# A recurrent attention with an MLP behind it: the first eight units in another order of instructions, loads and PSUM banks

## The chip, the cores and the metric

The kernel runs on one core of a Trainium2 chip. The metric is the device time of one execution in microseconds (us); of several runs the median is given. The engines are TensorE (PE; its weight loads are listed as PEld), VectorE (DVE), ScalarE (ACT), GpSimd (POOL) and SyncE (SP, which here only issues DMAs). Each engine works off its own list of instructions in order; semaphores tie the lists together. DMAs are issued from SP, ScalarE and GpSimd.

## The reference

Two stages. The first is a linear attention with a decaying state, for 4 batches, 8 heads, 768 steps and a head size of 48, in float32. The second is an MLP over the 3072 rows of 384 values that the first gives:

```python
for t in range(S):
    kt, vt, rt = k[:, :, t], v[:, :, t], r[:, :, t]
    cur = np.einsum('bhd,bhe->bhde', u[None] * kt, vt)
    y[:, :, t] = np.einsum('bhd,bhde->bhe', rt, state + cur)
    state = w[None, :, :, None] * state + np.einsum('bhd,bhe->bhde', kt, vt)
x = y.transpose(0, 2, 1, 3).reshape(B * S, H * D)      # 3072 x 384
h = x @ w_in                                            # 384 -> 2048
out = (h * sigmoid(h)) @ w_out                          # 2048 -> 384
```

## The kernel before

The 768 steps are cut into 6 chunks of 128. A unit is one chunk of one batch: 24 units, numbered chunk by chunk, so units 0 to 3 are chunk 0. For each unit the kernel does this:

- It loads r, k and v (192 KB each) into one of eight sets of buffers `rin`, `kin`, `vin` (`ld`, L71; `load`, L77). The heads are padded from 48 to 64 columns there; the pads are set to zero once.
- TensorE transposes r and k into PSUM (`turn`, L262), and VectorE multiplies them by powers of the decay on the way out (`decay_one`, L254: `rT`, `kT`).
- `product_pair` (L274) multiplies k by r for two units together, 64 small matmuls, into the four banks of the two PSUM tiles `att`. VectorE masks them into `am` (`masked`, L289). For odd units the halves are swapped, so `cast_v` (L236), which makes a 16-bit `v16` on ScalarE, also makes the crossed `vx` there.
- GpSimd makes the bonus of the step itself: `ku` = k times u (L209), `rku_f` = r times `ku` (L213); VectorE sums it per head (`bonus_sum`, L222), and GpSimd multiplies v by the sum (`bonus_v`, L227: `vu`).
- `outputs_y` (L295) adds up am times v in PSUM, and from chunk 1 on r times the state. `evict_y` (L332) adds `vu` on VectorE and writes `y16`.
- `outputs_s` (L309) and `state` (L336) bring the state on, with `kc`, the decayed k that GpSimd makes (`decayed_k`, L218), and with `sdec`, the decayed state, also from GpSimd (`decayed_state`, L325).
- `y16` is transposed into `xT`: for units 0 to 5 by TensorE and a copy on ScalarE (`turn_y`, `copy_x`), from unit 6 on by a DMA (`turn_y_dma`, L363).

The MLP works on chunks of 512 tokens. `l1` (L398) is a piece of the first layer: 128 or 256 of the 2048 hidden columns, three matmuls of 512 columns or six of 256, then the Silu on ScalarE into `gT`. `l2` (L420) is a piece of the second layer: four of the 16 matmuls of 384 columns that one batch's output takes; after the fourth piece it is evicted and stored. Pieces, the outputs of the attention and its transposed `y` share four PSUM banks, the tag "moe". The weights come in as four 384 KB pieces of `w_in` and four of `w_out` (16 bit, cast on the way), issued by GpSimd (`ld_win`, L83; `ld_wout`, L88).

The order of the work is written out by hand. For the first eight units, and the MLP of chunk 0, a string `order` (L485) names every step: `T0` is the transpose of unit 0, `A01` the product of 0 and 1, `Y0`, `S0` its outputs, `L0.2` and `G0.2` matmuls and Silu of a first-layer piece, `H0` a piece of chunk 1, `i_q0` and `i_o0` weight loads. Each engine gets its instructions in the order of the string. `4*T0` means four matmuls of zeros (`spin`, L158) ahead of `T0`. The string ends ahead of the product of 6 and 7. From there on, the loop at L518 takes two units at a time and puts pieces of the MLP from a list `fillers` between the attention's steps (`fill`, L448), 16 pieces a turn. The second layer of chunk 0 is the first thing in that list. SP also issues the stores.

The loads stand as follows in the lists: `w` as columns from SP and ScalarE; r0 on SP; k0 on ScalarE; `u`, spread over 128 partitions by the DMA (`u_bc`), on ScalarE; then r1, k1, v0, v1, and r, k, v of units 2 to 7 on SP, each behind the last.

Of the kernel before, what the change touches and what calls it, by code (L numbers as in the profile page):

```python
# [15 lines left out]
def kernel(  # L16
# [76 lines left out]
    def columns(eng, dst, src, j):  # L93
# [3 lines left out]
    w_row = cst.tile([1, HD], FP)  # L97
    ones = cst.tile([1, 128], FP)
# [6 lines left out]
    nc.scalar.dma_start(out=w_row, in_=bass.AP(tensor=w.tensor, offset=0, ap=[[0, 1], [1, HD]]))  # L105
    ld(0, rin, r)
    ld(0, kin, k, nc.scalar)
    nc.scalar.dma_start(out=u_bc, in_=bass.AP(tensor=u.tensor, offset=0,
                                              ap=[[0, 128], [D, H], [1, D]]))
    ld(1, rin, r)  # L110
    ld(1, kin, k)
    ld(0, vin, v)
    ld(1, vin, v)
    load(2)
    load(3)
# [25 lines left out]
    for i in range(NIN):  # L141
        nc.gpsimd.memset(kc[i][:, :, D:64], 0.0)
# [9 lines left out]
    def pads():  # L152
        for i in range(B, NIN):
            for dst in (rin, kin):
                nc.scalar.copy(out=dst[i][:, :, D:64],
                               in_=idle[:, 0:128].rearrange("p (h d) -> p h d", h=H))

    def spin(n):  # L158
        zs = ps.tile([128, 512], FP, name="zs", tag="moe", bufs=4)
        for _ in range(n):  # L160
            nc.tensor.matmul(zs, idle[:, 0:128], idle, start=True, stop=True)

    def clear():
        for t in att:
            for y in range(2):
                nc.tensor.matmul(t[:, y, :], idle[:, 0:128], idle, start=True, stop=True)
# [16 lines left out]
    def spread_w():  # L183
        spread["w"] = ps.tile([128, HD], FP, name="bc", tag="moe", bufs=4)
        nc.tensor.matmul(spread["w"], ones, w_row, start=True, stop=True)
# [4 lines left out]
    def powers_c():  # L190
        nc.scalar.activation(out=lamC.rearrange("p h d -> p (h d)"), in_=lnw_bc,
                             func=AF.Exp, scale=it_rev)
        nc.scalar.activation(out=wCT, in_=lnwT, func=AF.Exp, scale=float(C))
        nc.scalar.preload_act_table_set("silu_and_others")
# [14 lines left out]
    def bonus_ku(i):  # L209
        L(i)["ku"] = wrk.tile([128, H, D], FP, name="ku")  # L210
        nc.gpsimd.tensor_tensor(out=L(i)["ku"], in0=kin[i % NIN][:, :, 0:D], in1=u_bc, op=ALU.mult)  # L211

    def bonus_rku(i):  # L213
        L(i)["rku_f"] = wrk.tile([128, H, D], FP, name="rku_f")
        nc.gpsimd.tensor_tensor(out=L(i)["rku_f"], in0=rin[i % NIN][:, :, 0:D], in1=L(i)["ku"],  # L215
                                op=ALU.mult)
# [5 lines left out]
    def bonus_sum(i):  # L222
        L(i)["rku"] = wrk.tile([128, H], FP, name="rku")
        nc.vector.tensor_reduce(out=L(i)["rku"], in_=L(i)["rku_f"],  # L224
                                axis=mybir.AxisListType.X, op=ALU.add)

    def bonus_v(i):  # L227
        L(i)["vu"] = wrk.tile([128, H, D], FP, name="vu")
        nc.gpsimd.tensor_tensor(out=L(i)["vu"], in0=vin[i % NIN],  # L229
                                in1=L(i)["rku"].unsqueeze(2).broadcast_to([128, H, D]),  # L230
                                op=ALU.mult)
# [4 lines left out]
    def cast_v(i):  # L236
        v16 = L(i)["v16"] = L(i)["vy"] = wrk.tile([128, H, D], F16, name="v16", bufs=4)
        nc.scalar.copy(out=v16, in_=vin[i % NIN])  # L238
        if crossed(i):
            vx = L(i)["vy"] = wrk.tile([128, H, D], F16, name="vx", bufs=2)  # L240
            nc.scalar.copy(out=vx[0:HC], in_=v16[HC:C])
            nc.scalar.copy(out=vx[HC:C], in_=v16[0:HC])
# [10 lines left out]

    def decay_one(i, x):  # L254
        key, lam = (("rT", lamR), ("kT", lamK))[x]
        L(i)[key] = wrk.tile([PR, NP, C], FP, name=key)
        nc.vector.tensor_tensor(  # L257
            out=L(i)[key].rearrange("p g (y t) -> p y g t", y=2),
            in0=L(i)["t"][0:PR, :, x], in1=lam.rearrange("p g (y t) -> p y g t", y=2),
            op=ALU.mult)  # L260
# [34 lines left out]
    def outputs_y(i):  # L295
        sc, b = unit(i)
        yp = ps.tile([128, 512], FP, name="yp", tag="moe", bufs=4)
        L(i)["y"] = yp[:, 0:HD].rearrange("p (h d) -> p h d", h=H)
        for p in range(NP):
            if sc:  # L300
                nc.tensor.matmul(L(i)["y"][:, 2 * p:2 * p + 2, :],  # L301
                                 L(i)["rT16"][0:PR, p, :],
                                 st16[b][:, p, :], start=True, stop=False)
            for j in range(2):
                h = 2 * p + j
                nc.tensor.matmul(L(i)["y"][:, h, :], L(i)["am"][:, j, p, :], L(i)["vy"][:, h, :],  # L306
                                 start=not sc, stop=(not sc or j == 1))
# [24 lines left out]
    def evict_y(i):  # L332
        L(i)["y16"] = wrk.tile([128, H, D], F16, name="y16")
        nc.vector.tensor_tensor(out=L(i)["y16"], in0=L(i)["y"], in1=L(i)["vu"], op=ALU.add)  # L334
# [68 lines left out]

    def l2_mm(sc, b, part):
# [6 lines left out]
    def store(sc, b):  # L411
        osb = wrk.tile([128, HD], FP, name="osb", bufs=3)
        if sc < NCH - 1:
            nc.scalar.copy(out=osb, in_=opss[b])  # L414
        else:
            nc.vector.tensor_copy(out=osb, in_=opss[b])
        tt = b * S + sc * C
        nc.sync.dma_start(out=out[tt:tt + C, :], in_=osb)
# [34 lines left out]
    def second(sc):  # L453
        return [lambda b=b, p=p: l2(sc, b, p) for b in range(B) for p in range(4)]

    def rest_first(sc):
        return [lambda ft=ft: l1(sc, 2, 2, ft) for ft in range(0, NFT, 2)]

    def first(sc):
        return [lambda f=f: l1(sc, 0, B, f) for f in range(NFT)]  # L460
# [5 lines left out]
    def piece(word, f):  # L466
# [4 lines left out]
        "lnw": powers_r, "eK": exponents_k, "lamK": powers_k,  # L471
        "wb": spread_w,
        "lnwb": ln_w, "lamC": powers_c, "mx": cross_mask, "pads": pads, "clear": clear,
    }
    unit_steps = {
        "T": turn,
        "rT": lambda i: decay_one(i, 0), "kT": lambda i: decay_one(i, 1),
        "am": masked, "v16": cast_v, "kc": decayed_k,
        "vu": bonus_v,
        "Y": outputs_y, "S": outputs_s, "y16": evict_y, "yT": turn_y, "xT": copy_x,  # L480
        "st": state, "stb": state16, "ku": bonus_ku, "ru": bonus_rku, "rd": bonus_sum,
        "r16": cast_r, "sd": decayed_state, "i_q": ld_win, "i_o": ld_wout,
        "lr": lambda i: ld(i, rin, r), "lk": lambda i: ld(i, kin, k), "lv": lambda i: ld(i, vin, v),
    }
    order = """  # L485
        lnw eK lamK mx clear lr4 lk4 lv4 lr5 lk5 lv5 lr6 lk6 lv6 lr7 lk7 lv7 4*T0 ku0 rT0 kT0
        4*T1 rT1 kT1 v160 ru0 rd0 ku1 wb v161 A01 ru1 am0 rd1 vu0 lnwb i_q0 lamC pads am1 vu1
        4*Y0 y160 T2 kT2 2*Y1 y161 ku2 ru2 rT2 yT0 xT0 i_q1 yT1 xT1 v162 T3 kT3 rT3 ku3 ru3 rd2
        v163 4*A23 vu2 i_q2 rd3 vu3 am2 am3 L0.0 G0.0 L0.2 G0.2 Y2 y162 Y3 y163 kc0 yT2 xT2 L0.4
        G0.4 kc1 yT3 xT3 L0.6 G0.6 S0 st0 kc2 T4 kT4 rT4 kc3 L2.0 G2.0 S1 L2.2 G2.2 st1 ku4 v164  # L490
        L2.4 G2.4 S2 L2.6 G2.6 st2 ru4 i_q3 r164 L4.8 G4.8 S3 L4.9 G4.9 st3 rd4 ku5 L4.10 G4.10
        T5 kT5 rT5 L4.11 G4.11 vu4 ru5 i_o0 A45 rd5 am4 r165 v165 L4.12 G4.12 vu5 kc4 L4.13
        G4.13 am5 sd4 kc5 Y4 S4 y164 st4 L4.14 G4.14 sd5 i_o1 Y5 S5 y165 st5 L4.15 G4.15 yT4 xT4
        yT5 xT5 T6 kT6 rT6 ku6 ru6 i_o2 H0 H1 v166 r166 H2 H3 T7 kT7 rT7 ku7 i_o3 v167 r167 H4
        ru7 rd6 stb4 stb5
    """
    for word in order.split():
        if "*" in word:
            n, word = word.split("*")
            spin(int(n))  # L500
        if word[0] == "A":
            product_pair(int(word[1]))
        elif word in steps:
            steps[word]()
        elif word[0] == "L":
            piece(word[1:], l1_mm)
        elif word[0] == "G":
            piece(word[1:], l1_silu)
        elif word[0] == "H":
# [3 lines left out]
    load(8)  # L513
    load(9)
    fillers.extend([lambda ft=ft: l1(1, 0, 2, ft) for ft in range(10, NFT, 2)])
    fillers.extend(second(0))

    for i in range(B + 2, NU, 2):  # L518
        sc, b = unit(i)
        nxt = range(i + 2, min(i + 4, NU))  # L520
        product_pair(i)
        if i > B + 2:
            for n in nxt:
                bonus_products(n)
                decayed_k(n)
        if i > B + 2:
            masked(i)
            masked(i + 1)
        else:
            bonus_v(i)  # L530
            decayed_k(i)
            decayed_state(i)
            masked(i)
            bonus_sum(i + 1)
            masked(i + 1)
            bonus_v(i + 1)
            decayed_k(i + 1)
            decayed_state(i + 1)
            for n in nxt:
                bonus_products(n)  # L540
                decayed_k(n)
        fill(4)
# [11 lines left out]
        if b:  # L554
            fillers.extend((first(sc) if sc > 1 else rest_first(sc)) + second(sc))
# [46 lines left out]
```

## Time and profile before

| | us |
|---|---|
| median of 5 runs | 194.95 |
| lowest, highest | 194.43, 197.03 |
| the five runs | 197.03, 196.82, 194.43, 194.74, 194.95 |
| the profiled execution | 197.03 |
| its span, first to last instruction | 195.2 |
| mean granted TensorE clock | 0.983 |

All the profile's lines are of the one profiled execution. Its views are read like this. The page gives busy time of each engine, with its share of the span and the number of its instructions, and then the span in 40 slices of 4.9 us, where a digit is the busy share in tenths; PEclk is the clock that TensorE was granted, in tenths. The chain of waits goes back from the last instruction, at each step to what released it; its rows are start, length, engine and line, and "issue" is time in which the engine waited for nothing that the profile shows. A row of groups has line, engine, operation, result and operands, count, busy time and mean ns of one. For a DMA the trace has the issue and the time to landing.

The landing times of the first loads, from issue and time to landing, are these (us):

| load | issue | landed |
|---|---|---|
| r0 (SP) | 1.43 | 4.9 |
| k0 (ScalarE) | 2.00 | 5.9 |
| `u_bc` (ScalarE) | 2.44 | 8.4 |
| r1 | 1.9 | 8.6 |
| k1 | 2.52 | 9.3 |
| v0, v1 | 3.41, 6.0 | 10.1, 10.9 |
| r2, v2 | 8.54, 10.04 | 12.3, 14.2 |
| k4, k5 | 15.32, 20.74 | 21.5, 28.8 |
| k7 | 30.77 | 38.5 |
| `w_in` pieces | 13.30, 18.72, 22.70, 30.17 | 19.5, 23.8, 28.4, 36.3 |
| `w_out` pieces | 36.73, 41.80, 44.66, 46.43 | 41.8, 48.7, 51.5, 54.8 |

### The profile page before, as it was taken

How to read it: one execution, taken by the hardware profiler on the slowest of the kernel's cores; microseconds unless marked ns; L12 is line 12 of the kernel's file. 1: busy time of each engine (PE TensorE's matmuls, PEld its weight loads, DVE VectorE, ACT ScalarE, POOL GpSimd, SP SyncE). 2: the span in 40 equal slices, each digit the busy share in tenths (PEclk: the TensorE clock that was granted, in tenths of full speed). 3: DMA queues.
4: the chain of work that ended last, by engine and by line, in shares of the span. 5: the costliest groups of instructions: out<-in, count | busy, mean ns of one | idle time of the engine just before them, and what ended most of it. 6: DMA issues, size and time to landing. Idle time of an engine off the chain costs nothing.

```text
span 195.2 us, 5626 instructions
## 1 busy us (share of the span) xinstructions
PE 185.3 (95%) x2306; PEld 119.7 (61%) x2306; DVE 102.7 (53%) x188; ACT 108.4 (56%) x212; POOL 120.3 (62%) x159
## 2 busy tenths in 40 slices
PE   7598989889999999999999999999999999999994
PEld 2365776567866786665556665556665556644563
DVE  6248769784663663772772782772673364200120
ACT  5285558758653286067684076792186791179300
POOL 8287995899999957938929919929829430000000
PEclk9966999999999999999999999999999999999999
DMA  4999999999839629349359158359278111320022
GB/s 82 174 201 186 199 196 169 184 203 194 129 82 178 187 52 213 104 106 181 84 111 217 56 126 169 80 97 208 60 161 187 24 20 44 81 81 0 3 81 81
DMA packets 90267, 24.35 MB, mean 125 GB/s; under 512 B 83329, under 2 KB 90242, under 8 KB 90242
## 3 DMA queue, kind: packets, MB, share of 16 engines
q1 hardware_dynamic: 84992, 20.39, 48.2%
q0 software_dynamic: 3712, 3.15, 11.0%
q10 hardware_dynamic: 1538, 0.46, 1.4%
q8 instruction: 18, 0.29, 0.6%
q14 instruction: 7, 0.06, 0.1%
HBM read 20.65 MB, written 4.72 MB: 130 GB/s over the span
## 4 chain that ended last, share of the span: by engine, by line
PE 75%; POOL 13%; issue 4%; DMA 3%; ACT 2%; ACTq 0%; DVE 0%; POOLq 0%
PE ops L408 31%; PE hps L387 26%; PE att L284 7%; PE att L251 4%; POOL ku L211 3%; DMA u_bc<-in_u_dram 3%; POOL kc L219 3%; POOL rku_f L215 2%; POOL vu L229 2%; PE yp L306 2%; PE yp L301 2%; POOL win L84 2%; PE sp L318 1%; PE ops L433 1%; ACT gT L395 1%
## 5 line engine op out<-in xcount | busy, mean ns | idle before, releaser
L387 PE MATMUL hps<-xT,win 128*128 128x512 f16 (+1 forms) x360 | 68.2, 337 | 0.7 <-ACT xT L376 0.5
L395 ACT ACTIVATE gT<-hps 128x512 f16<-128x512 f32 x96 | 56.2, 598 | 20.0 <-PE hps L387 17.9
L408 PE MATMUL ops<-wout,gT 128*128 128x384 f16 x368 | 64.0, 326 | 0.0
L408 PEld LDWEIGHTS <-gT 128*128 128x128 f16 x368 | 34.7, 98 | 22.2
L387 PEld LDWEIGHTS <-win 128*128 128x128 f16 x360 | 33.2, 98 | 24.2 <-issue 1.1
L229 POOL TENSOR_TENSOR vu<-vin,rku 128x384 f32<-128x384 f32 x24 | 19.8, 829 | 30.6 <-DVE rku L224 27.3
L414 ACT COPY osb<-ops 128x384 f32<-128x384 f32 x20 | 9.6, 478 | 43.4 <-PE ops L408 39.7
L291 DVE TENSOR_TENSOR am<-att,maskM 128x1024 f16<-128x1024 f32 x12 | 14.7, 1224 | 35.2 <-PE att L284 35.2
L211 POOL TENSOR_TENSOR ku<-kin,u_bc 128x384 f32<-128x384 f32 x24 | 24.1, 1006 | 3.5 <-DMA u_bc<-in_u_dram 3.3
L215 POOL TENSOR_TENSOR rku_f<-rin,ku 128x384 f32<-128x384 f32 x24 | 24.1, 1004 | 1.7
L219 POOL TENSOR_TENSOR kc<-kin,lamC 128x384 f16<-128x384 f32 x24 | 23.9, 1001 | 0.0
L284 PEld LDWEIGHTS att<-rT,kT 48*64 48x64 f32 x768 | 19.1, 140 | 6.4 <-issue 4.5
L257 DVE TENSOR_TENSOR rT<-att,lamR 112x512 f32<-112x512 f32 x24 | 16.4, 684 | 12.0 <-PE att L251 4.4
L284 PE MATMUL att<-rT,kT 48*64 48x128 f32 (+1 forms) x768 | 21.8, 257 | 1.0 <-DVE rT L257 0.8
L334 DVE TENSOR_TENSOR y<-yp,vu 128x384 f16<-128x384 f32 x24 | 13.3, 556 | 14.1 <-issue 4.8
L257 DVE TENSOR_TENSOR kT<-att,lamK 112x512 f32<-112x512 f32 x24 | 16.4, 681 | 3.6 <-PE att L251 3.5
L291 DVE TENSOR_TENSOR am<-att,maskX 128x1024 f16<-128x1024 f32 x12 | 14.6, 1214 | 0.0
L238 ACT CAST v<-vin 128x384 f16<-128x384 f32 x24 | 11.4, 511 | 4.4 <-DMA vin<-in_v_dram 4.4
L329 POOL TENSOR_TENSOR sdec<-st,wCT 112x384 f32<-112x384 f32 x16 | 13.2, 826 | 0.0
L224 DVE TENSOR_REDUCE rku<-rku_f 128x8 f32<-128x384 f32 x24 | 12.3, 542 | 0.6 <-POOL rku_f L215 0.6
L272 ACT CAST rT<-rT 112x512 f16<-112x512 f32 x20 | 12.4, 619 | 0.3 <-DVE rT L257 0.2
L306 PEld LDWEIGHTS <-am 128*128 128x128 f16 x192 | 10.0, 98 | 3.9 <-DVE am L291 1.7
(64 smaller groups left out, 161.3 us busy)
## 6 DMA issues: line engine op xcount, KB each, us to landing
rin<-in_r_dram SPq DMA_DIRECT2D x24, 192.0 KB, 3.8
vin<-in_v_dram SPq DMA_DIRECT2D x24, 192.0 KB, 4.2
kin<-in_k_dram SPq DMA_DIRECT2D x23, 192.0 KB, 4.0
out_dram<-osb SPq DMA_DIRECT2D x23, 192.0 KB, 2.2
win<-in_moe_w_in_dram POOLq DMA_DIRECT2D x4, 384.0 KB, 5.9
wout<-in_moe_w_out_dram POOLq DMA_DIRECT2D x4, 384.0 KB, 6.9
xT<-y SPq DMA_TRANSPOSE x18, 2.3
kin<-in_k_dram ACTq DMA_DIRECT2D x1, 192.0 KB, 3.9
```

The source lines that it names most:

```text
L211: nc.gpsimd.tensor_tensor(out=L(i)["ku"], in0=kin[i % NIN][:, :, 0:D], in1=u_bc, op=ALU.mult)
L215: nc.gpsimd.tensor_tensor(out=L(i)["rku_f"], in0=rin[i % NIN][:, :, 0:D], in1=L(i)["ku"], op=ALU.mult)
L219: nc.gpsimd.tensor_tensor(out=kc[i % NIN][:, :, 0:D], in0=kin[i % NIN][:, :, 0:D], in1=lamC, op=ALU.mult)
L229: nc.gpsimd.tensor_tensor(out=L(i)["vu"], in0=vin[i % NIN], in1=L(i)["rku"].unsqueeze(2).broadcast_to([128, H, D]), op=ALU.mult)
L257: nc.vector.tensor_tensor(out=L(i)[key].rearrange("p g (y t) -> p y g t", y=2), in0=L(i)["t"][0:PR, :, x], in1=lam.rearrange("p g (y t) -> ...
L284: nc.tensor.matmul(a[e][o0:o0 + HC, j, p, c0:C], kT[r0:r0 + D, p, s0:s0 + HC], rT[r0:r0 + D, p, c0:C], start=True, stop=True)
L291: nc.vector.tensor_tensor(out=am.rearrange("p h g c -> p (h g) c"), in0=L(i)["a"].rearrange("p h g c -> p (h g) c"), in1=(maskX if crossed ...
L306: nc.tensor.matmul(L(i)["y"][:, h, :], L(i)["am"][:, j, p, :], L(i)["vy"][:, h, :], start=not sc, stop=(not sc or j == 1))
L334: nc.vector.tensor_tensor(out=L(i)["y16"], in0=L(i)["y"], in1=L(i)["vu"], op=ALU.add)
L387: nc.tensor.matmul(hps[:, f, :], win[:, q, (ft + f) * 128:(ft + f + 1) * 128], xts[sc][:, q, b0:b0 + nb, :].rearrange("p b t -> p (b t)"), ...
L395: nc.scalar.activation(out=gts[sc][:, ft:ft + m, b0 * C:(b0 + nb) * C], in_=hpss[b0, ft], func=AF.Silu)
L408: nc.tensor.matmul(opss[b], gts[sc][:, ft, b * C:(b + 1) * C], wout[:, ft, :], start=(ft == 0), stop=(ft == NFT - 1))
```

## The change

The order of the first eight units is new, and with it what can stand there.

- Loads: `u` comes as one row and is spread by a matmul, like `w`. The string itself names every load. r, k and v of units 0 to 5 come first; then all the weights; r, k and v of units 6 to 9 come behind a memset on GpSimd that writes into r6's buffer (`hold_rows`), so that SP's next load has to wait for it.
- Order: the products of 0 and 1, 2 and 3, 4 and 5 all stand ahead of the MLP but for one piece. The string now also has the whole second layer of chunk 0 (`M`), and ends behind the product of 6 and 7.
- PSUM: chunk 0's second layer adds up in the banks of `att` (`front_mm`). r and k of units 2, 3, 6 and 7 are transposed into the four "moe" banks (`turn_ring`), r and k apart.
- Units 0 to 3: `vu` is added by a float32 matmul with the identity (`add_bonus`) into a PSUM bank that a matmul of zeros opens, and ScalarE evicts (`evict_y`).
- Small things: `spin` is gone, `clear` has six zero matmuls in place of four. The pads of `kc` are set by VectorE, in the string, and no longer by GpSimd ahead of it; those of `rin` and `kin` 4 to 7 by GpSimd, no longer by ScalarE. The table load for Silu is a step of its own. More buffers for `ku`, `rku_f`, `rku`, `vu`, `v16`, `vx`, `rT`, `kT`, `y16` and `osb`.
- In the loop: the casts of units 6 and 7 stand in its first turn, and the first layer goes by pairs of batches (256 columns) in every chunk, added to `fillers` each turn.

```diff
-    nc.scalar.dma_start(out=w_row, in_=bass.AP(tensor=w.tensor, offset=0, ap=[[0, 1], [1, HD]]))
-    ld(0, rin, r)
-    ld(0, kin, k, nc.scalar)
-    nc.scalar.dma_start(out=u_bc, in_=bass.AP(tensor=u.tensor, offset=0,
-                                              ap=[[0, 128], [D, H], [1, D]]))
-    ld(1, rin, r)
-    ld(1, kin, k)
-    ld(0, vin, v)
-    ld(1, vin, v)
-    load(2)
-    load(3)
+    for dst, src in ((u_row, u), (w_row, w)):
+        nc.scalar.dma_start(out=dst, in_=bass.AP(tensor=src.tensor, offset=0, ap=[[0, 1], [1, HD]]))
+        if src is u:
+            ld(0, rin, r)
+            ld(0, kin, k, nc.scalar)
...
-    for i in range(NIN):
-        nc.gpsimd.memset(kc[i][:, :, D:64], 0.0)
+    for i in range(B, NIN):
+        nc.gpsimd.memset(rin[i][:, :, D:64], 0.0)
+        nc.gpsimd.memset(kin[i][:, :, D:64], 0.0)
...
+    def kc_pads():
+        for i in range(NIN):
+            nc.vector.memset(kc[i][:, :, D:64], 0.0)
+
+    def hold_rows(i):
+        nc.gpsimd.memset(rin[i][:, :, 32:64], 0.0)
...
     def clear():
-        for t in att:
-            for y in range(2):
-                nc.tensor.matmul(t[:, y, :], idle[:, 0:128], idle, start=True, stop=True)
+        for n in range(6):
+            zeros(att[n % 4 // 2][:, n % 2, :])
...
+    def copy_u():
+        nc.vector.tensor_copy(out=u_bc.rearrange("p h d -> p (h d)"), in_=spread["u"])
...
+    def turn_ring(i, x):
+        t = L(i)["t", x] = ps.tile([128, NP, C], FP, name="tr", tag="moe", bufs=4)
+        flat = (rin, kin)[x][i % NIN].rearrange("p h d -> p (h d)")
+        for p in range(NP):
+            nc.tensor.transpose(t[0:PR, p, :], flat[:, 128 * p:128 * p + PR], ident)
...
+        if not sc:
+            nc.tensor.matmul(L(i)["yf"], idle[:, 0:128], idle[:, 0:HD], start=True, stop=False)
...
+    def add_bonus(i):
+        nc.tensor.matmul(L(i)["yf"], ident, L(i)["vu"].rearrange("p h d -> p (h d)"),
+                         start=False, stop=True)
...
+        if i < B:
+            nc.scalar.copy(out=L(i)["y16"], in_=L(i)["y"])
+        else:
+            nc.vector.tensor_tensor(out=L(i)["y16"], in0=L(i)["y"], in1=L(i)["vu"], op=ALU.add)
...
+    def front_acc(b):
+        return att[b // 2][:, b % 2, 0:HD]
+
+    def front_mm(b, part):
+        for ft in range(4 * part, 4 * part + 4):
+            nc.tensor.matmul(front_acc(b), gts[0][:, ft, b * C:(b + 1) * C], wout[:, ft, :],
+                             start=(ft == 0), stop=(ft == NFT - 1))
...
+    def second(sc, b0):
+        return [lambda b=b, p=p: l2(sc, b, p) for b in (b0, b0 + 1) for p in range(4)]
+
+    def first(sc, b0, f0=0):
+        return [lambda ft=ft: l1(sc, b0, 2, ft) for ft in range(f0, NFT, 2)]
...
     order = """
+        clear lr1 lk1 lk2 lnw lk3 eK ub lv0 lv1 lamK lr2 mx lr3 Tr0 ubc Tr1 lr5 rT0
+        Tk0 ku0 lv5 Tk1 rT1 lr4 ku1 kT0 Tk2 lv3 lv2 kT1 ru0 lk4 kT2 A01 ku2 lk5 rd0
+        lv4 kcm ru1 v161 wb q0 am0 Tr2 v160 vu0 lnwb am1 Y0 ku3 lamC Tk3 Tr3 rT2 ru2
+        V0 v165 kT3 Y1 ru3 rT3 silu rd1 A23 kc0 rd2 rd3 vu1 y160 v162 am2 vu2 V1 v163
+        yT0 vu3 am3 Y2 V2 q1 y161 T4 y162 kc1 yT1 xT0 rT4 T5 xT1 kT4 Y3 kc4 S0 V3 rT5
+        q2 yT2 y163 kT5 L0.2 q3 st0 yT3 G0.2 A45 o0 r165 xT2 kc2 S1 r164 L0.0 st1 o1
+        xT3 L0.4 G0.0 kc3 L2.0 v164 S2 G0.4 L0.6 o2 st2 G2.0 L2.2 ku4 G0.6 L2.6 G2.2
+        sd6 S3 L2.10 G2.6 st3 ru4 L2.8 G2.10 L2.4 sd7 rd4 L0.10 G2.4 am5 o3 L4.12 G2.8
+        sd4 L4.13 G4.12 am4 G0.10 L0.8 ku5 G4.13 L4.15 kc5 G0.8 Y4 S4 G4.15 M2.0 st4
+        ru5 Y5 M1.0 stb4 rd5 S5 sd5 M0.0 M2.1 vu4 st5 M3.0 stb5 y164 M0.1 hold6 vu5
+        lr6 M1.1 lk7 y165 L4.14 lk6 M1.2 G4.14 lr7 yT4 lk8 M1.3 lv7 M0.2 lk9 ku7 M0.3
+        lv6 M2.2 lv9 osb0 ku6 lv8 M2.3 lr8 ru7 yT5 Tr6 Tk6 xT5 lr9 xT4 kc6 M3.1 rT6
+        osb1 osb2 Tr7 Tk7 rd7 kT6 vu7 M3.2 rT7 ru6 M3.3 kT7 H0 osb3 rd6 A67
     """
...
-    load(8)
-    load(9)
-    fillers.extend([lambda ft=ft: l1(1, 0, 2, ft) for ft in range(10, NFT, 2)])
-    fillers.extend(second(0))
+    fillers.extend(first(1, 0, 2) + second(1, 0))
...
-        product_pair(i)
         if i > B + 2:
-            for n in nxt:
-                bonus_products(n)
-                decayed_k(n)
+            product_pair(i)
...
+        if i > B + 2:
+            fill(4)
+        else:
+            for n in (i, i + 1):
+                cast_v(n)
+                cast_r(n)
+                fill(2)
...
-        if b:
-            fillers.extend((first(sc) if sc > 1 else rest_first(sc)) + second(sc))
+        fillers.extend(first(sc, b) + second(sc, b))
```

## The prediction

> **What bounds the kernel now.** I read the page's first two parts, then the chain of waits in order of time, then busy times in stretches of 2 us, then each DMA's issue with its time to landing.
>
> ```profile
> span 195.2 us, 5626 instructions
> PE 185.3 (95%) x2306; PEld 119.7 (61%) x2306; DVE 102.7 (53%) x188; ACT 108.4 (56%) x212; POOL 120.3 (62%) x159
> ...
> PEclk9966999999999999999999999999999999999999
> ```
>
> TensorE looks busy for 95% of the span, but that counts the zero products of `spin` and matmuls at half clock. The chain shows where TensorE really sets the pace:
>
> ```profile
> 2.44 5.88 DMA u_bc<-in_u_dram
> ...
> 8.46 0.99 POOL ku L211
> ...
> 32.00 2.95 issue
> 34.99 0.83 POOL vu L229
> ...
> 48.32 1.55 PE att L284 x54
> 49.88 2.07 PE hps L387 x18
> 51.95 0.65 PE ops L408 x4
> ...
> 56.31 1.04 PE att L251 x32
> ...
> 171.54 10.40 PE hps L387 x48
> 181.93 7.80 PE ops L408 x48
> 189.73 2.65 PE ops L433 x32
> ```
>
> Up to 41 us the chain runs over GpSimd, which starts at 8.46 because `u_bc` lands late. From 48.32, the product of units 6 and 7, to 192.4 it is TensorE without a gap: 144.1 us, then 2.8 us of eviction and store. So there are two questions: how much TensorE work is left when that product starts, and when it starts.
>
> ```profile
> 10.00:12.00 2.00, 1.82 (x22) 1.04 (x25) 1.66 (x3) 1.60 (x4) 1.92 (x3) 0.81 1.07 211
> 12.00:14.00 2.00, 2.00 (x52) 1.89 (x44) 0.00 (x0) 1.93 (x5) 2.00 (x3) 0.50 0.95 183
> 14.00:16.00 2.00, 2.00 (x13) 0.84 (x12) 1.87 (x3) 1.99 (x6) 0.32 (x2) 0.50 1.06 170
> 16.00:18.00 2.00, 2.00 (x24) 1.28 (x22) 2.00 (x3) 0.71 (x4) 1.92 (x3) 0.50 1.09 168
> 18.00:20.00 2.00, 1.45 (x32) 1.08 (x30) 1.16 (x3) 0.97 (x3) 1.98 (x3) 0.99 1.23 240
> ```
>
> Columns: stretch, its length, busy PE, PEld, DVE, ACT, POOL (instructions), granted clock, DMA share, GB/s. From 11.2 to 18 the clock is half although TensorE is busy all the time; it comes back after spins at 14.0 and 17.2.
>
> **Work behind the product of 6 and 7.** A first-layer piece is 0.65 us (48 matmuls of 512 columns in 10.40; by pairs, 12 of 256 columns in 1.31, so 0.655), a second-layer piece of four matmuls 0.65. After the change all 16 second-layer pieces of chunk 0 lie ahead of it (-10.4), four of the five early first-layer pieces of chunk 1 fall behind it (+2.6), and 64 pieces go by pairs (+0.3): 144.1 - 7.5 = 136.6. So the product may start at 48.3 + 7.5 = 55.8 without loss; each us later is a us lost.
>
> **The loads.** In the trace r0 lands at 4.9 and v2, the tenth transfer, at 14.2: 1.03 us each. `u` now comes as one 1.5 KB row, spread by a matmul (0.91, the row of `bc`) and a VectorE copy (0.56), both beside idle engines. So the first `ku` starts at 6.0, when k0 is there, not 8.46. In the new order v5 is the 12th and k5 the 17th transfer: 4.9 + 11 x 1.03 = 16.3 and 21.4. The first weight load, issued by GpSimd at about 12, puts 1.9 us between (384 KB at the 205 GB/s that weights alone reach at 48 to 51 us), the second some of the same: v5 at 18.3, k5 between 23.4 and 25.
>
> **The spins.** 18 zero products of `spin` go (6.7 us busy), `clear` gets two more. Those in TensorE's waits gave nothing but the clock. Without them I expect half clock from about 8 us. A product of two units then takes 2.8 us (60 matmuls in 2.83 at 11.26) in place of 1.5, two units' turns 2.2 in place of 1.04. The trace doesn't show when the clock returns without spins: between 13 us and the first window filled by the MLP, some 5 us after its start. I take the middle twenties, since the new bonus products use all rows.
>
> The Trainium skill ("TensorE: Matmul & The Clock Gate", Part 1) has the full clock granted after one busy window of about 3.4 us. The rows speak against it as it stands: 2.00 of 2.00 busy from 12 to 16 us at 0.50. By the rule the clock would be back by 18 and the product of 6 and 7 would start near 54.5; by the rows as below.
>
> **New work on TensorE.** Four bonus products (`add_bonus`, 384 columns, f32): the trace has this shape only in `bc`, 0.91 with its latency; bounds 0.65 and 1.8; I take 0.65 at full and 1.3 at half clock. They wait for GpSimd's `vu`, with turns and outputs queued behind on TensorE; `vu` of 0 to 3 end at 13.8, 18.6, 19.4 and 20.2, each before TensorE gets there, so the wait costs nothing. Four zero matmuls ahead of the outputs: 0.16 to 0.32 each. ScalarE evicts those four units (0.48 each) in place of VectorE (0.56). The pads of `kc` go from GpSimd (1.23 in all) to VectorE, between the first bonus sum and the first mask, where VectorE waits for the product anyway; without that cover they cost 1.2. The pads of `rin`, `kin` go from ScalarE (15.0 to 16.7) to GpSimd, idle there until 6.0.
>
> **Walk to the MLP.** Tk2 ends at 9.7, the product of 0 and 1 at half clock at 12.6, w's spread and r2's turn at 14.0, Y0 at 15.0 (ScalarE casts v0 until 14.2), turns of unit 3 and the bonus at 17.5, Y1 at 18.3, the product of 2 and 3 at 21.1 (19 at full clock). On ScalarE v5's cast and crossing (18.3 to 19.9) and the table load (1.28) stand ahead of y0's eviction: 21.7. Queued behind it are v2's and v3's casts with crossing, then y1's eviction at 24.3. TensorE waits for these in yT0, Y2, yT1 and for k5 in T5. With full clock from 25, T5 ends at 26.3, and Y3, S0, the last bonus, yT2, a first-layer piece, yT3 and the product of 4 and 5 (0.45 + 0.25 + 0.65 + 0.35 + 0.65 + 0.35 + 1.5 = 4.2) give 30.5.
>
> **MLP to the product of 6 and 7.** 15 first-layer pieces 9.8, 16 second-layer pieces 10.4, five state products 0.85, two outputs 0.76, turns 1.4, one piece of chunk 1 0.65: 23.85, so 54.35 if nothing waits. Weights don't: GpSimd issues them at about 20, 23, 24, 25, 26, 28 and 38, and at 1.9 us each all but the last are there by 36; the last lands by 43 to 46 (5.1 to 8.4 to landing in the trace) and is used at 47.7. The banks of `att` don't: the last `osb` copy (0.48) lies beside the piece of chunk 1. GpSimd does: the state evictions of unit 3 (four at 0.32) end at 36.7, then come 0.83 + 0.8 + 0.83 + 3 x 1.0 + 0.5 + 0.83 + 0.83 + 0.5 + 0.2 up to the memset of `hold_rows`: 45. SP's first load of chunk 1's second half waits for it, and all loads and the four stores are queued behind. r6 lands at 48.9 (3.8), r7 third after it at 51.9. GpSimd's `rku_f` of 7 ends at 52.9, VectorE's sum at 53.5, then three decays at 0.61: the product starts at 55.4.
>
> **Behind it.** The casts of units 6 and 7 (v16 0.51 twice, crossing 1.02, rT16 0.62 twice) now stand between ScalarE's Silus of the loop's first pieces; before, ScalarE had them behind it by 48. Four pieces take TensorE 2.6 us; with four PSUM buffers the fifth waits for the third's Silu, behind 3.3 us of casts and three Silus of 0.6. I take a stall of 1.5, bounds 0 and 2.2. Later iterations have nine pieces and the turns (6.9 us) between an output and its first use, against five and 4.4 before with no wait: nothing.
>
> **Sum.** 55.4 + 1.5 + 136.6 + 2.8 = 196.3 us, 1.1 over the span. The profiled execution took 197.03, 1.83 over its span and 2.08 over the median of the five runs (194.43 to 197.03, in two groups). Taken as it stands the sum gives 198.1; as a difference to the median, 196.1. What made the profiled run longer the trace doesn't tell; I take the middle, 197.1.
>
> **Rivals.**
> Faster: the clock is back by 18 and rows land at 0.75 us, as the four from r1 to v1 did (8.6 to 10.9, three steps in 2.25). k5 is there by 21 (16.9, and two weight loads at 1.9), the product of 4 and 5 ends at 28, the one of 6 and 7 starts at 52, ScalarE's stall is hidden: 52 + 136.6 + 2.8 = 191.4, so 193.2 or 191.3, in the middle 192.3. It decides from a start before 53.5. For it: GpSimd starts 2.5 us sooner and the weights come 6 to 15 us sooner. Against: the clock rows, and 190 GB/s shared with the weights.
>
> Much slower: the clock returns only inside the MLP. The walk at half clock: bonus products 1.3, turns 1.1, outputs 0.85 each, the product of 4 and 5 from 32.2 to 35.0, then 23.85 and at least one us of slow MLP: 60. Span 60 + 1.5 + 136.6 + 2.8 = 200.9, so 202.7 or 200.7, about 201.7. For it: 11.2 to 14.7, a whole product and 0.6 us of spin, did not bring the clock back.
>
> No effect: TensorE waits in T5, but sooner (29), GpSimd's chain moves with it, the stall is half: 54 + 0.7 + 136.6 + 2.8 = 194.1, so 195.9 or 193.9, about 194.9.
>
> **How the numbers follow.** About 1% is what a measurement of this kernel can tell from no change. Forecast 0.38 (own range 195.3 to 199; 0.24 of it slower, 0.14 within 1%), much slower 0.24, no effect 0.14 (0.09 within, 0.05 faster), faster 0.24 (0.20 faster, 0.04 within). Together faster 0.25, within 0.27, slower 0.48. A range from 191.8 to 202.5 leaves a tenth at each end.
>
> **What would show it.** The start of the product of 6 and 7 against 55.8; the granted clock in 8 to 30 us; k5's landing and the end of the product of 4 and 5 against 30.5; r7's landing against 51.9 and what ends the wait of that product (a decay, if GpSimd's chain is late); ScalarE's Silus and TensorE's idle just behind it. I would be wrong if that product starts before 53.5, or if the later iterations wait for `xT`.

## The result, and the profile after

The changed kernel took 196.76 us (median of 43 runs, 195.68 to 197.47), the kernel before 195.24 beside it (80 runs, 193.93 to 197.37): a ratio of 1.0078, 95% interval 1.0063 to 1.0093. It is 0.8% slower, less than the 1% that the prediction set as what can be told apart. The prediction was 197.1 (191.8 to 202.5). All ratios leave out the executions that took over 1.5% more than the fastest of the same kernel.

The profiled execution took 197.4 us, with a span of 195.6. These are the lines of its page that answer to those of before:

```profile
span 195.6 us, 5942 instructions
...
PE 188.9 (97%) x2476; PEld 143.8 (74%) x2476; DVE 102.1 (52%) x193; ACT 110.2 (56%) x208; POOL 120.7 (62%) x160
...
PEclk9999999999999999999999999999999999999999
```

The clock's row shows no cut. The chain of waits of the same execution, in order of time (start, length, engine, line):

```profile
9.56 3.42 PE att L293 x62
12.98 1.57 PE bc L180 x2
...
17.98 1.28 PE yp L322 x2
...
19.90 1.72 PE att L293 x64
...
27.82 1.50 PE att L293 x64
...
53.33 0.67 PE hps L406 x6
54.04 0.47 issue
54.51 0.48 ACT osb L445
55.04 1.57 PE att L293 x64
...
58.06 0.60 ACT gT L414
58.66 0.41 ACT v L238
59.09 0.51 ACT vx L241
59.61 0.51 ACT vx L242
60.14 0.62 ACT rT L281
60.76 0.51 ACT gT L414
61.31 0.82 PE hps L406 x6
...
190.04 2.65 PE ops L464 x32
```

Three things are to be seen. GpSimd, which carried the chain up to 41 us before, is gone from it: from 9.56 on the chain is TensorE (94% of the span in all), but for one mask on VectorE at 21.64 and the two holes below. Its first product takes 3.42 us, not 1.5, and a bonus product 1.28, where later ones take 0.73: TensorE runs at half speed up to about 20 us. Of the 3.42, 0.6 are a wait inside the product: its weight loads go on at 10.15, when VectorE has k of unit 1 decayed. The other 2.83 are the time of the half-speed product in the kernel before. And behind dense work up to 54 us there are two holes, both made by ScalarE: the output copy `osb` ahead of the product of units 6 and 7, and the casts of 6 and 7 behind it.

TensorE's busy time in the same stretches of 2 us as before (stretch, its length, busy PE, PEld, DVE, ACT, POOL, granted clock, DMA share, GB/s):

```profile
10.00:12.00 2.00, 2.00 (x40) 1.85 (x40) 1.75 (x11) 1.23 (x3) 2.00 (x3) 1.00 1.11 219
12.00:14.00 2.00, 2.00 (x32) 1.28 (x28) 0.97 (x1) 0.81 (x2) 1.98 (x4) 1.00 1.15 193
14.00:16.00 2.00, 2.00 (x13) 1.29 (x13) 1.76 (x3) 1.20 (x3) 1.93 (x3) 1.00 1.13 173
16.00:18.00 2.00, 2.00 (x15) 2.00 (x13) 1.00 (x2) 1.60 (x4) 0.80 (x1) 1.00 0.97 184
18.00:20.00 2.00, 2.00 (x15) 0.97 (x18) 1.98 (x4) 1.69 (x2) 0.75 (x1) 1.00 0.82 163
```

TensorE is busy throughout and the granted clock says 1.00, yet the instructions take twice their later time. The column is no proof of full speed; the durations are.

The product of 6 and 7 starts at 55.04, before the break-even of 55.8. Behind it lie 137.65 us of TensorE to 192.69, then 2.9 us. By these two profiles the kernels are as good as equal (spans of 195.6 and 195.2); the medians are 1.5 us apart.

### The profile page after: what moved, and what is told of

It is laid out like the page before. It is cut to its first block, busy times and chain, and to the rows that moved or that the text cites. A ratio compares the mean times of both kernels' runs of the same rounds, so it can differ in the third digit from the quotient of the medians.

```text
span 195.6 us, 5942 instructions
## 1 busy us (share of the span) xinstructions
PE 188.9 (97%) x2476; PEld 143.8 (74%) x2476; DVE 102.1 (52%) x193; ACT 110.2 (56%) x208; POOL 120.7 (62%) x160
## 4 chain that ended last, share of the span: by engine, by line
PE 94%; ACT 2%; DVE 2%; issue 1%; DVEq 0%
PE hps L406 32%; PE ops L439 26%; PE att L293 10%; PE att L251 6%; PE att L428 5%; PE yp L318 3%; PE tr L258 2%; PE yp L313 2%; PE sp L334 2%; PE bc L180 2%; PE att L157 1%; PE yp L322 1%; PE ops L464 1%; DVE rT L266 1%; DVE am L300 1%; ACT gT L414 1%
## 5 line engine op out<-in xcount | busy, mean ns | idle before, releaser
L406 PE MATMUL hps<-xT,win 128*128 128x256 f16 (+1 forms) x564 | 70.0, 275 | 0.6 <-DVE y L353 0.5
L406 PEld LDWEIGHTS <-win 128*128 128x128 f16 x564 | 53.2, 98 | 9.2 <-issue 0.9
L439 PE MATMUL ops<-wout,gT 128*128 128x384 f16 x304 | 52.4, 326 | 0.0
L439 PEld LDWEIGHTS <-gT 128*128 128x128 f16 x304 | 29.1, 98 | 18.1
L353 DVE TENSOR_TENSOR y<-yp,vu 128x384 f16<-128x384 f32 x20 | 11.1, 557 | 16.2 <-PE yp L318 5.4
L266 DVE TENSOR_TENSOR rT<-att,lamR 112x512 f32<-112x512 f32 x20 | 13.7, 686 | 9.6 <-PE att L251 9.5
L445 ACT COPY osb<-ops 128x384 f32<-128x384 f32 x16 | 7.6, 478 | 17.9 <-PE ops L439 17.9
L266 DVE TENSOR_TENSOR kT<-att,lamK 112x512 f32<-112x512 f32 x20 | 13.5, 679 | 0.0
L364 DVE TENSOR_TENSOR st<-sp,sdec 48x192 f32<-48x192 f32 x32 | 11.2, 351 | 2.6 <-POOL kc L219 1.6
L373 POOL CAST stb<-st 112x384 f16<-112x384 f32 x16 | 8.1, 505 | 7.2 <-DVE st L364 7.0
```

The costliest lines, as they stand in the source:

```text
L266: nc.vector.tensor_tensor(out=L(i)[key].rearrange("p g (y t) -> p y g t", y=2), in0=L(i)["t"][0:PR, :, x], in1=lam.rearrange("p g (y t) -> ...
L406: nc.tensor.matmul(hps[:, f, :], win[:, q, (ft + f) * 128:(ft + f + 1) * 128], xts[sc][:, q, b0:b0 + nb, :].rearrange("p b t -> p (b t)"), ...
L439: nc.tensor.matmul(opss[b], gts[sc][:, ft, b * C:(b + 1) * C], wout[:, ft, :], start=(ft == 0), stop=(ft == NFT - 1))
```

## The experiments

Theory from this profile: the change takes TensorE's waits for GpSimd away and pays for it at three places: `osb` 1.06, casts 0.9, and the half clock. Rivals: the bonus products' time, the held-back rows, or GpSimd's chain, each of which might set the end as well. Ratios are to the kernel before on the same chip; the changed kernel's own is 1.0078.

**The copy ahead of the product.** In the string, `H0` stands for matmuls and Silu, so the copy behind it in ScalarE's list waits for the Silu:

```diff
-        osb1 osb2 Tr7 Tk7 rd7 kT6 vu7 M3.2 rT7 ru6 M3.3 kT7 H0 osb3 rd6 A67
+        osb1 osb2 Tr7 Tk7 rd7 kT6 vu7 M3.2 rT7 ru6 M3.3 kT7 osb3 H0 rd6 A67
```

> Only the last output copy of chunk 0 (osb3) moves ahead of the first-layer piece H0 in the order; the changed kernel's ratio to before is 1.0078. Theory (TensorE is the bound, and its wait of 1.06 us ahead of the product of 6 and 7 is the copy queued behind H0's Silu on ScalarE): the product starts at 54.0 in place of 55.0 and the time falls by 0.8 to 1.1 us, ratio 1.003. Rival A (GpSimd's chain behind the held loads is just as late): the decays of 7 end the wait instead, the gain is under 0.3 us, ratio 1.007. Rival B (the casts behind the product eat it): the product starts a microsecond sooner, but the sixth piece waits a microsecond longer, ratio 1.007.

195.74 us, ratio 1.0025 (0.9998 to 1.0052): 1.0 us less than the changed kernel. ScalarE's instructions in the changed kernel show why (start, length, line, operation, in brackets the idle time and its releaser):

```profile
51.19 0.48 ACT L445 COPY osb<-att 128x384 f32<-128x384 f32 x1 [0.28 <-PE att L428]
54.02 0.60 ACT L414 ACTIVATE gT<-hps 128x512 f16<-128x512 f32 x1 [2.35 <-PE hps L406]
54.51 0.47 ACT L445 COPY osb<-att 128x384 f32<-128x384 f32 x1
```

ScalarE idles for 2.35 us waiting for the piece, while the sum that the copy needs is ready at about 53.3. With the copy first, TensorE runs without a gap from 52.40 into the product at 53.15. From the start of the product of 4 and 5 to this one lie 26.15 us, 27.28 in the changed kernel. The loss is the order of two instructions on an idle engine.

**The casts.**

```diff
-        osb1 osb2 Tr7 Tk7 rd7
+        osb1 osb2 r166 v167 Tr7 Tk7 rd7
...
-            for n in (i, i + 1):
-                cast_v(n)
-                cast_r(n)
-                fill(2)
+            cast_v(i)
+            cast_r(i + 1)
+            fill(4)
```

> Only the cast and crossing of v7 and the cast of rT6 move from the loop's first turn to ScalarE's idle time ahead of H0. Theory (ScalarE's casts between the first Silus stall TensorE behind the product of 6 and 7): the idle of 0.9 us between 56.6 and 62.0 goes, time -0.6 to -0.9 us, ratio 1.004. Rival (the wait only moves, to v6 or to the state): under 0.3 us, ratio 1.007.

196.17, ratio 1.0043 (1.0016 to 1.0070): 0.6 us less. From the product's start to the next turns TensorE now needs 8.0 us (53.68 to 61.69) in place of 8.9; `osb` still costs 1.06. The span of this profile is 193.3, 2.3 below the changed kernel's, and only 0.9 of that are the casts. The rest comes from the front: TensorE is back at full speed at about 17.4, not 20 (the transpose of r3 at 16.92 takes 0.80 us, 1.06 in the changed kernel), so the product of 4 and 5 starts at 26.40, not 27.76. Nothing was changed there; the moment moves from execution to execution. So what an edit is worth has to be read within one profile, or from many times.

**Both.** The two diffs together.

> Both edits together: osb3 ahead of H0, and v16, vx of 7 and rT16 of 6 cast ahead of the loop. Theory (two separate losses of TensorE, the wait ahead of the product of 6 and 7 and the stall behind it, 1.06 and 0.9 us in the changed kernel's trace): the two gains add up, as 1.0078 less 0.0053 less 0.0035 from the single runs: 0.999, from 0.996 to 1.001. Rival (GpSimd's chain, whose last decay ends at 53.05 in the changed kernel, holds the product as soon as ScalarE does not): only the larger of the two is gained, 1.002 to 1.005, and a VectorE decay is named as releaser of that product.

195.29, ratio 1.0026 (0.9994 to 1.0057). By the medians that is 1.5 us less than the changed kernel, of 1.6 from the single runs, but those are from different chips; by the ratio it is no better than the copy alone (1.0025), and in the rival's range. The theory's 0.999 fell just outside the interval. ScalarE's instructions:

```profile
52.00 0.51 ACT L241 COPY vx<-v 64x384 f16<-64x384 f16 x1
52.52 0.51 ACT L242 COPY vx<-v 64x384 f16<-64x384 f16 x1
53.06 0.48 ACT L445 COPY osb<-att 128x384 f32<-128x384 f32 x1
```

The moved casts now stand ahead of the copy and hold it to 53.06; TensorE waits 0.24 for it. No decay of VectorE is named, so GpSimd's chain does not bind. From the product's start to the next turns it is 8.0 us again. So in the profile both gains are there (0.8 and 0.9); that the times add up is not shown.

**The bonus on VectorE again.** Left out are `V0` to `V3` and the zero matmuls in `outputs_y`; VectorE adds `vu` when it evicts:

```diff
-        if i < B:
-            nc.scalar.copy(out=L(i)["y16"], in_=L(i)["y"])
-        else:
+        if True:
             nc.vector.tensor_tensor(out=L(i)["y16"], in0=L(i)["y"], in1=L(i)["vu"], op=ALU.add)
```

> One part undone: the bonus of units 0 to 3 is added by VectorE at the eviction again; the four float32 products with the identity (1.28 and three of 0.72 us on TensorE) and the four zero products (about 1 us in all) are gone. Theory (TensorE is the bound from 9.6 us on, so what it does there is paid for): the product of 4 and 5 starts 1 to 1.5 us sooner (26.3 to 26.8 in place of 27.8) and the time falls by as much, ratio 1.000 to 1.003. Rival (loads, VectorE and ScalarE stand right behind TensorE there): VectorE gets 2.2 us more ahead of the masks, no gain or up to 1 us slower, ratio 1.007 to 1.013.

196.16, ratio 1.0054 (1.0020 to 1.0089), between the two. TensorE's instructions behind the product of 2 and 3:

```profile
20.72 0.34 PE L387 MATMUL yT<-ident,y 128*128 128x128 f16 x3
22.12 0.37 PE L316 MATMUL yp<-v,am 128*128 128x48 f16 x8 [1.06 <-DVE am L300]
...
23.71 0.50 PE L387 MATMUL yT<-ident,y 128*128 128x128 f16 x3 [0.63 <-DVE y L349]
```

A part of what TensorE no longer does, it waits, and it waits for VectorE: 1.06 us for the mask of unit 2 and 0.63 for the eviction of y1, which VectorE starts at 23.11, when it is done with the masks of 2 and 3. GpSimd had `vu` ready at 21.33. In the changed kernel a bonus product lies beside that mask, and 0.16 us of wait is left.

The product of 4 and 5 starts at 27.43 against 27.76, but that is no price of the bonus: the half speed lasts longer here (the product of 2 and 3 takes 2.88 us from 17.91), and the granted clock is cut to 0.50 from 23.5 to 26.9. By the times the bonus on TensorE costs some 0.6 us, less than the theory had, and the intervals of the two ratios overlap.

**Zero products ahead of the product of 0 and 1.**

```diff
-        for n in range(6):
+        for n in range(8):
...
-        ... Tr0 ubc Tr1 lr5 rT0
+        ... Tr0 ubc Tr1 z3 lr5 rT0
-        Tk0 ... kT0 Tk2 lv3 ...
+        Tk0 ... kT0 Tk2 z5 lv3 ...
```

> Zero products are put back into TensorE's waits: eight in place of six in the first step, three behind the turn of r1, five ahead of the product of 0 and 1. Theory (half clock from 4 to 20 us costs, since TensorE is the bound): the product of 0 and 1 takes 1.5 in place of 3.4 us, the product of 4 and 5 starts 1.5 to 2.6 us sooner, ratio 0.995 to 1.001. Rival (v2, landed at 20.2, VectorE and ScalarE are the bound there, so the clock is nearly free): the product of 0 and 1 is as short, but the product of 4 and 5 starts less than 0.7 us sooner, ratio 1.005 to 1.008. If the clock does not rise, the zeros only cost: ratio above 1.008.

195.58, ratio 1.0045 (1.0012 to 1.0078): some gain, but short of the theory's range. TensorE's instructions:

```profile
9.84 0.65 PE L263 MATMUL tr<-ident,kin 128*112 128x128 f32 x4
10.33 1.24 PE L166 MATMUL zs<-idle 128*128 128x512 f16 x5
11.50 1.95 PE L298 MATMUL att<-rT,kT 48*64 48x128 f32 x64
...
20.82 0.36 PE L323 MATMUL yp<-v,am 128*128 128x48 f16 x8 [0.38 <-ACT v L243]
```

The transpose of k2 takes 0.65 us, 1.10 in the changed kernel, and the product 1.95 instead of 3.42: full speed is back at about 10. The product of 4 and 5 starts at 26.14, 1.6 sooner, as the theory had it. But with the casts moved and no zeros added it started at 26.40, with full speed from 17.4 on: 7 us more of full speed, less the zeros' own time, gave 0.26. The time saved meets v2, which lands at 20.2, as in the changed kernel; ScalarE's cast waits 1.43 us for it, and TensorE 0.38 for the cast.

**All three.**

> The same two edits, and the eight zero products ahead of the product of 0 and 1. Theory (the half clock up to about 19 us is the third loss; what is won there reaches the end as long as TensorE is dense from the MLP on): the 0.0033 of the run with zero products alone come on top, 0.996, from 0.992 to 0.998, below the kernel before; the product of 4 and 5 at about 26.2. Rival (with TensorE sooner, GpSimd's chain of the second half of the MLP or the late rows of units 2 and 3 bind): as without the zero products, 0.998 to 1.001.

195.49 (193.45 to 197.71), ratio 1.0018 (0.9977 to 1.0058). No clear gain over the run without zeros; the theory's 0.992 to 0.998 is not borne out. In this profile the same zero products did not bring full speed before about 12.8 us; the moment differs from run to run. The times of this version scatter more than those of any version above (by 4.3 us, the changed kernel's by 1.8).

**The rows not held back.** `hold6` is left out of the string.

> The changed kernel without the memset that holds the rows of units 6 to 9 back; nothing else. They then go out of SP as soon as their buffers and SP are free, beside the weights. Theory (hold_rows keeps 2.3 MB of rows out of the way of 3 MB of weights, and does not bind itself: the product of 6 and 7 was held by ScalarE): weights land later, TensorE waits in the first or second layer of chunk 0, slower than the changed kernel, 1.010 to 1.030. Rival A (the weights have enough slack, the rows were not late): as the changed kernel, 1.005 to 1.010. Rival B (the rows behind the memset were what set the product of 6 and 7): 1.000 to 1.005.

197.04, ratio 1.0142 (1.0095 to 1.0189), in the theory's range, at its low end. TensorE now waits for a weight piece:

```profile
29.54 1.48 PE L406 MATMUL hps<-xT,win 128*128 128x256 f16 x12 [0.57 <-DMA win<-in_moe_w_in_dram]
```

That piece was issued at 22.18 and landed 7.3 us later, against 4.8 in the changed kernel. Between the products of 4, 5 and of 6, 7 lie 28.0 us in place of 27.3. By the profiles, holding the rows back is worth 0.7 us; the ratios say 0.6%, 1.2 us, with intervals that only just part.

**The kernel before without `spin`.**

```diff
-        lnw eK lamK mx ... 4*T0 ku0 rT0 kT0
-        4*T1 rT1 kT1 ...
-        4*Y0 y160 T2 kT2 2*Y1 ...
-        ... 4*A23 ...
+        lnw eK lamK mx ... T0 ku0 rT0 kT0
+        T1 rT1 kT1 ...
+        Y0 y160 T2 kT2 Y1 ...
+        ... A23 ...
```

> The kernel before without its 18 zero products of spin; nothing else. Theory (they did keep up the clock, so taking them out is a cost of the change): matmuls of 10 to 20 us at half speed, products of 2.8 in place of 1.5 us; up to 41 us the chain goes over GpSimd, so part of that is hidden: 1.003 to 1.012. Rival A (all hidden behind GpSimd and the loads): 0.998 to 1.003. Rival B (the 6.7 us of zero products were in the way themselves): 0.985 to 0.998.

198.44, ratio 1.0201 (1.0153 to 1.0248): more than any of the three theories allowed. TensorE's products of 0, 1 and of 2, 3 are both at half speed:

```profile
10.53 2.84 PE L284 MATMUL att<-rT,kT 48*64 48x128 f32 x64
...
20.74 2.83 PE L284 MATMUL att<-rT,kT 48*64 48x128 f32 x60 [0.77 <-DVE rT L257]
```

So without `spin` the kernel before takes 1.7 us longer than the changed kernel (1.2% by the ratios, each to the kernel before on its own chip). Among kernels without `spin` the new order gains; with `spin`, the kernel before stays ahead.

**The kernel before again, for its profile**, twice.

> The kernel before itself, unchanged, for a second profile. Its times lie in two groups, 193.5 to 195.5 and 196 to 197.4; the profile on record is of the upper group (197.03). Theory (the groups differ by the half clock behind the first product: 11.2 to 18 us in the profile on record): where this profiled execution is of the lower group, the product of 0 and 1 or all matmuls behind it up to 18 us run at full speed, and the product of 6 and 7 starts 1.5 to 3 us before 48.3, at 45.3 to 46.8. Rival (the groups differ further behind, or in loads): the front is as on record and the product starts at 48 again. Ratio 0.998 to 1.002 by both.

> The kernel before once more, for a profile of the lower group (194 to 194.8), since both profiles so far (197.03 and 197.35) were of the upper one, with two different fronts: full speed and then half from 11.2 to 18 us, and half speed from 3.4 to 16 us. Theory (the groups differ by the half speed alone): in an execution of 194 to 194.8 the product of 0 and 1 and what follows run at full speed, the product of 2 and 3 ends 2.5 to 3 us before 22.9 to 23.3, and that of 6 and 7 starts some 25.4 us after that end, at 45.3 to 46.2. Rival (they differ elsewhere): the product of 2 and 3 ends at 22.5 to 23.5 again.

Ratio 1.0005 (0.9973 to 1.0037). Both profiled executions are of the upper group again (197.35 and 196.6 us), so the theory on the lower group stays untested. In both, the product of 0 and 1 is at half speed; here that of the second:

```profile
11.00 2.84 PE L284 MATMUL att<-rT,kT 48*64 48x128 f32 x64
...
20.55 2.04 PE L284 MATMUL att<-rT,kT 48*64 48x128 f32 x64
```

In all three profiles of the kernel before the product of 6 and 7 starts 25.4 us after the end of that of 2 and 3 (22.93 and 48.32; 23.31 and 48.71; 22.52 and 47.90). Up to there the front sets the time. The spans are 195.2, 195.6 and 194.8: the changed kernel's 195.6 is among them, and the 1.5 us between the medians come from executions of the kernel before at 194 to 195, which no profile shows. That these have full speed early is likely (without `spin` there are none: 197.96 to 198.76), not shown.

**How long until full speed.** `clear` with 20 zero matmuls in place of six.

> The changed kernel with 20 zero products in clear in place of six: 128 rows by 512 columns each, without a gap from 1.29 us. Measures how long TensorE must be busy for the full clock: the zeros go from 0.43 to 0.21 us where it is granted. Theory (a few us of unbroken use of all rows bring it): the step lies inside the zeros, between 4.5 and 8.5 us; everything behind starts some 2 us later but at full speed, 0.998 to 1.006. Rival (a fixed time after the start, not TensorE's use, or the use of fewer rows counts as well): no step inside the zeros, half speed up to 10 us and more, 1.007 to 1.015.

197.46 (195.53 to 199.83), ratio 1.0063 (1.0039 to 1.0087), between the two ranges. The zeros alone, by the us (stretch, its length, busy PE with the number of matmuls, PEld, granted clock, DMA share, GB/s):

```profile
5.00:6.00 1.00, 1.00 (x4) 0.35 (x3) 1.00 1.27 258
6.00:7.00 1.00, 1.00 (x4) 0.39 (x3) 1.00 1.19 237
7.00:8.00 1.00, 1.00 (x7) 0.47 (x5) 1.00 1.00 202
```

The step lies at 7.0 us, 5.7 us after the first zero, inside the zeros as the theory had it. Full speed is not kept. In the stretches of this execution, columns as above, the granted clock is cut later on:

```profile
10.00:12.00 2.00, 1.24 (x20) 0.92 (x20) 1.24 (x3) 1.67 (x4) 1.97 (x3) 1.00 1.02 202
12.00:14.00 2.00, 1.19 (x26) 0.95 (x30) 2.00 (x4) 0.38 (x1) 2.00 (x4) 0.92 1.09 219
14.00:16.00 2.00, 2.00 (x46) 1.88 (x41) 1.11 (x10) 0.00 (x0) 1.98 (x3) 0.50 1.10 213
...
20.00:22.00 2.00, 2.00 (x30) 1.54 (x31) 1.86 (x4) 1.93 (x3) 0.52 (x2) 0.87 0.79 158
```

TensorE is then waiting for rows and decays (1.24 and 1.19 of 2 us busy). Five of the ten executions took 198.8 to 199.8, the others, from which the ratio is, 195.5 to 196.1. Full speed at 7 us is no gain if TensorE has nothing dense to do behind it.

**The best version.** Casts, copy and zero products as above, with two more edits: the casts of 7 behind `osb3`, and v2, v3 loaded ahead of r4, k4, r5, k5, v5 (with v5's cast moved behind `xT1`).

```diff
-        osb1 osb2 r166 v167 Tr7 Tk7 ... kT7 osb3 H0 rd6 A67
+        osb1 osb2 r166 Tr7 Tk7 ... kT7 osb3 v167 H0 rd6 A67
...
```

> The version with osb3, casts and zero products, improved: osb3 now ahead of the crossing casts of 7 (in the run of both edits these casts held osb3 and TensorE for 0.24 us), and v2, v3 loaded ahead of r4, k4, r5, k5, v5 (the zero products had moved TensorE up to the wait for v2). Theory: no idle time ahead of the product of 6 and 7, TensorE 0.5 to 1.5 us sooner at the product of 4 and 5 than 26.4; ratio 0.990 to 0.998, below both kernels. Rival (k5 and the turns of 5 bind instead of v2, and the clock's return still scatters): 0.998 to 1.003, as the last version.

193.99 us (eight runs, 191.77 to 197.14); the kernel before took 194.75 (25 runs, 193.81 to 195.87), the changed one 196.76. The ratio is 0.9888 (0.9843 to 0.9933), without the three runs over 196; all 25 of the kernel before lie below 196, so it flatters. The medians of all give 0.996. All waits of TensorE from 4 to 60 us in its profile (who, for whom, us in total, times, longest):

```profile
PE yT L396 <- ACT y L356: 0.3, 1, 0.3
PE att L298 <- DVE rT L269: 0.2, 1, 0.2
PE yp L323 <- DVE am L305: 0.2, 1, 0.2
```

No wait at the product of 6 and 7, which starts at 52.96. But that of 4 and 5 starts at 26.81, not sooner as the theory had it: v5, now among the last loads, lands at 24.4, and its cast stands ahead of y3's eviction, the 0.3 us above. And in this execution full speed came only at about 12.8 us. The version beats the changed kernel clearly (0.996 against 1.0078 even with all runs); that it beats the kernel before hangs on which runs are counted.

## Why the prediction was right

The likeliest case, a little slower by the lost clock and by ScalarE's casts, is what came. By the prediction's own bound of 1%, though, 0.8% is no change, to which it gave 0.27, and not slower, to which it gave 0.48. Its terms by the changed kernel's profile:

- **Break-even, 55.8.** Right. Work behind the product was summed as 136.6 + 1.5; measured 137.65.
- **Loads.** Too slow by 1 to 2 us: v5 at 16.3, not 18.3, k5 at 22.4, not 23.4 to 25. The product of 4 and 5 ended at 29.32, not 30.5.
- **Clock.** Full speed at about 20 us: later than the rule's 18, sooner than the middle twenties. In four further kernels with the same front it lay between 17 and 19. The row of granted clock, from which the prediction meant to read it, stayed at 1.00; it had to be read from durations. In the changed kernel's front this moment is worth 1.4 us (full speed at 17.4 or at 20).
- **The bonus on TensorE.** Costed in full (0.65 to 1.3 each). It costs TensorE that, 1.28 for the first, but the run without it shows that TensorE would wait for VectorE instead of a part of it.
- **The start of the product of 6 and 7: 55.4 predicted, 55.04 measured, and the step failed.** "The last `osb` copy (0.48) lies beside the piece of chunk 1" was costed at nothing. It lies behind that piece, in ScalarE's list behind its Silu: 1.06 us, shown by the exchange of the two. The chain named in its place, GpSimd's, was 2.4 us earlier than said: the memset ran at 43.25, not 45, r7 landed at 49.25, not 51.9, and the last decay ended at 53.05. One error hid the other.
- **Behind it.** The mechanism was right, the size not: 0.9 us, not 1.5. The casts moved ahead took the stall out of the profile and gave 0.6 in the median.
- **Later turns.** A turn of the loop takes 14.29 us, 14.24 before: 0.4 in all by pairs, 0.3 predicted, and TensorE's chain shows no wait for `xT`.
- **`spin`.** "Those in TensorE's waits gave nothing but the clock": true, but that clock was not priced against the kernel before. Its profile was of an execution at 197.03 that had been cut to half from 11.2 to 18 us, and so had little of what `spin` buys. The run without `spin` puts it at 3.9 us in the median.
- **The offset.** The sum gave a span of 196.3 (195.6 measured), 1.1 over before's. Against the median this left a choice between 198.1 and 196.1; the middle fitted, since the sum was 0.7 too high and the profile of before lay further above its median than the profile after does above its own (2.1 and 0.6). That was luck in size, not insight. In the faster rival 191.3 should be 191.2 (191.4 less the 0.25 by which the span lay above the median); nothing hangs on it.

So the change does what it says: GpSimd leaves the path and the waits go. What it gains is given back as half speed up to 20 us and two waits for ScalarE. The waits are shown by their removal, 1.06 and 0.9 us in the profiles. The half speed is priced in the kernel before: leaving out `spin` alone costs 2.0%, and the rest of the change gains 1.2% on that, which leaves the 0.8%. In the changed kernel it is not priced, since no run had full speed there at will.

## What to carry to other kernels

A step that contains two engines' work (matmuls and Silu) hides an order: when a copy is put "beside" it, look in the list of the copy's engine for what stands ahead of it. Before products that look idle are taken out, measure the kernel without them alone; and where runs of a kernel spread over more than the effect, find out which end of the spread the profile is from before its stalls are priced. A cost that fills a wait for another engine (the bonus on TensorE beside VectorE's mask) is worth less than its length when it is removed. And where the front of a kernel shifts by itself from execution to execution, compare lengths within a profile, not starts between two.

## What was unexpected of the hardware

Half speed shows in two ways. At the start, matmuls of 512 columns came 0.43 us apart with a granted clock of 1.00 in the rows, for 5.7 us of unbroken zeros, and the half speed lasted up to 17 to 20 us in the changed kernel's front. Later cuts are recorded as 0.50. By the share of each stretch at half clock they lasted 6.8 us twice (11.2 to 18.1 in the kernel before, 13.7 to 20.5 with 20 zeros) and 3.4 us once (23.5 to 26.9 with the bonus on VectorE). No idle time of TensorE in the 5 us ahead of these cuts was longer than 1.3 us. Between the first full speed at 7.0 and the cut at 13.7 lie 6.7 us.

The Trainium skill ("TensorE: Matmul & The Clock Gate", Part 1) describes a free-running window of 3.4 us; by that figure, as an estimate, these are two, two, one and two windows. Its one busy window before full speed is less than the 5.7 us measured here; the two agree only if the window that counted ran from 3.6 to 7.0, some 2.3 us after the first zero.

The same zero products ahead of the first product ended at full speed at about 10 us in one profile and not before about 12.8 in two others, so the moment differs from run to run.
